# Attention's matmuls between those of the first product, and D^T G one step later

## The chip, the cores and the metric

The kernel runs on one core of one Trainium2 chip. The metric is the device time of one execution in microseconds (us). The kernel before takes 780.31 us in the median of 3 runs (776.99 to 781.22).

## The reference

```
attention, per batch and head, in chunks of 64 positions:
    scores = q_c @ k_c.T / sqrt(D);  scores -= max(scores, -1)
    attn = exp(scores) / (sum + 1e-9);  out = attn @ v_c
x = out as (4608, 512)
first layer:   h = max(x @ w_in, 0);  x = (h * h) @ w_out       (512 -> 2048 -> 512)
soft mixture:  logits = x @ phi                                 (32 slots, 8 experts)
    d = softmax over tokens;  slot_input = d.T @ x
    slot_out = max(slot_input @ w1[e], 0) @ w2[e]
    c = softmax over slots;   result = c @ slot_out
```

There are 8 batches, 8 heads, 576 positions and a head size of 64.

## The kernel before

The 4608 tokens are 36 tiles of 128 tokens (two chunks of 64). The tiles form blocks: one of 1, one of 2, then eleven of 3. A block goes through 16 steps, one for each strip of 128 columns of the first layer.

A step of block b and strip f does this: the first product, 12 matmuls of 384 columns in fp16 parts (`moe_h`, tile hps), relu and square on ACT, and, two steps later, three transpositions of the squares (`moe_turn`, gT), their copy out of PSUM into a tile G (`moe_keep`), and after every fourth strip the logits (`moe_logits`, L). The second layer is never formed by itself: w_out is folded into phi beforehand, and d.T @ x is got as D^T G, where G are the transposed squares. `soft(b)` is a generator that runs one stretch per step after a block's last logits: scaled logits (Ls), their sum (the product at L864, called l4), softmax over tokens (dts), softmax over slots, then the transposition of dts (L917) and dd (L919), and in the next step D^T G (L926, 24 rows of the trace), which is added to acc (L937).

The attention of tile i is a table of operations (`attention(i)`), each with an engine, the operations that it needs and a stage. In the order of time, with the names used below: loads of q, k, v (SyncE); `am`, the largest magnitudes (DVE L182); the reduction over partitions (PE L205, L206, called r1 below); scales (DVE L215, L218, L398); `hi` (ACT L405) and `lo` (DVE L410), the fp16 parts of q and k; T, a DMA transpose into qkT (L431); `vh` and `vl`, the parts of v (GpSimd L420, DVE L425); `qbd`, two copies of qkT (DVE L435); scores `qk`, 24 matmuls of 64 columns (L446 to L448); `mx` (DVE L452), `less` (DVE L455), exp (ACT L461), `su` (DVE L466), `rs` (DVE L468); normalisation (GpSimd L471); the parts of the probabilities (ACT L481, GpSimd L484); PT, a DMA transpose into pT (L487); the values product `pv`, 24 matmuls of 64 columns (L498 to L500); `xh` (ACT L504) and `xl` (DVE L510), the parts of the result in xb, the operand of the first product. Buffers come in pairs by the tile's parity, so the loads of tile i+2 wait until tile i is done with its own: v's until the second `vl`, q's until `hi` and `lo`.

Up to some 175 us a list scheduler in the kernel sets the order of all engines. Then the steady part begins. A tile's table is handed out by tokens: at step st + k its operations of stage k are written down, ahead of that step's first product. `st` is the tile's block's first step less 16, and 5 less for each tile that follows in the block. On TensorE the written order is the program's order:

```
        put_until(t + 1)
        ...
            moe_h(b, f)
            moe_relu(b, f)
            moe_square(b, f)
        ...
        for fn in slots.pop(t, []):
            fn()
```

On the other engines a scheduler at build time orders the instructions, and each engine works through its queue in that order. Of the eight banks of PSUM two are for hps, one for gT, two for logits (one of them later for gT as well), and three, called misc, are shared in turn by the attention and `soft`.

Of the kernel before, what the change touches and what calls it, by code (L numbers as in the profile page):

```python
# [37 lines left out]
N32 = 9  # L38


class Op:
# [9 lines left out]
        self.share = 0.0  # L51

    def __call__(self):
        self.fn(self.eng) if self.choose else self.fn()


def cost_of(kind, n):
# [17 lines left out]
def kernel(  # L75
# [25 lines left out]
    dve, act, pool, pe, sp = nc.vector, nc.scalar, nc.gpsimd, nc.tensor, nc.sync  # L101

    blocks = []
# [62 lines left out]
    ps_t = ps1.enter_context(tc.tile_pool(name="ps_t", bufs=1, space=PSUM))  # L166
    ps_h = ps1.enter_context(tc.tile_pool(name="ps_h", bufs=2, space=PSUM))
    ps_m = ps1.enter_context(tc.tile_pool(name="ps_m", bufs=1, space=PSUM))
    bank_of, n_misc, turn, held_banks = {}, [0], [None], {}

    def misc():
        x = bank_of.get(turn[0])
        if x is None:
            while n_misc[0] % 3 in held_banks:
                n_misc[0] += 1
            x = n_misc[0] % 3
            n_misc[0] += 1
        return ps_m.tile([P, 512], F32, tag=f"misc{x}", name="misc")

    def largest_of(src, am):  # L180
# [189 lines left out]
    def attention(i):  # L370
        b, j = tile_block[i]
# [6 lines left out]
        v, ops = {}, {}  # L378

        def old(*names):  # L380
            return [(("t", i - 2), n) for n in names]

        older = old
# [56 lines left out]
        def scores():  # L440
            qkT, qbd = qkT_b[par], qbd_b[par]
            kh = qkT[:, 8:12].rearrange("p a (h2 t) -> p (a h2) t", h2=2)
            kl = qkT[:, 12:16].rearrange("p a (h2 t) -> p (a h2) t", h2=2)
            v["sc"] = sc = misc().rearrange("p (h t) -> p h t", h=8)
            for h in range(8):
                pe.matmul(sc[:, h], qbd[:, 0, h], kh[:, h], start=True, stop=False)  # L446
                pe.matmul(sc[:, h], qbd[:, 0, h], kl[:, h], start=False, stop=False)
                pe.matmul(sc[:, h], qbd[:, 1, h], kh[:, h], start=False, stop=True)  # L448

        def largest():  # L450
            v["mx"] = sm.tile([P, 8], F32, tag="mx", name="mx", bufs=2)
            dve.tensor_reduce(out=v["mx"], in_=v["sc"], axis=AX.X, op=ALU.max)  # L452
# [36 lines left out]
        def pv():  # L489
            vbd, pT = vbd_b[par], pT_b[par]  # L490
            v["xq"] = misc()
            v["xp"] = xp = v["xq"].rearrange("p (a t) -> p a t", a=4)
            for y in range(8):
                c, hp = divmod(y, 4)
                o = xp[:, hp, 64 * c : 64 * c + 64]
                ph = pT[:, y // 2, 64 * (y % 2) : 64 * (y % 2) + 64]
                pl = pT[:, 4 + y // 2, 64 * (y % 2) : 64 * (y % 2) + 64]
                pe.matmul(o, vbd[:, 0, y], ph, start=True, stop=False)  # L498
                pe.matmul(o, vbd[:, 0, y], pl, start=False, stop=False)
                pe.matmul(o, vbd[:, 1, y], ph, start=False, stop=True)  # L500


        def xh():
# [43 lines left out]
        for c in range(2):  # L547
            ops[f"qd{c}"] = Op("dve", 0.44, ["T", *old("qk")], 6, lambda c=c: qdiag(c))
        ops["qk"] = Op("pe", 0.75, ["qd0", "qd1"], 8, scores)
        ops["max"] = Op("dve", 0.6, ["qk"], 8, largest)  # L550
        ops["less"] = Op(
            "dve", 0.6, ["max", *(old("phi", "plo") if i - 2 >= N32 else older("Tp"))], 8, less
        )
        ops["exp"] = Op("act", 0.72, ["less"], 9, exp)
        ops["sums"] = Op("dve", 1.03, ["exp"], 9, sums)
        ops["normal"] = Op({"pool": 1.2, "dve": 0.61}, None, ["sums"], 9, normal)
        ops["phi"] = Op({"act": 0.63, "pool": 0.8}, None, ["normal", *old("PT")], 10, phi_)
        ops["plo"] = Op("pool", 1.25, ["phi"], 10, plo)
        ops["PT"] = Op("dma", 0.9, ["plo", *old("pv")], 10, ptrans)
        ops["pv"] = Op("pe", 0.75, ["PT", "vl0", "vl1"], 14, pv)  # L560
        ops["xh"] = Op("act", 0.6, ["pv"], 14, xh)
        ops["xl"] = Op("dve", 0.6, ["xh"], 14, xl)
        for n in ("lo0", "lo1", "vl0", "vl1", "qd0", "qd1", "normal"):
            ops[n].share = 0.4
        return ops
# [150 lines left out]
    def cols(b):  # L716
        o0 = bank0.get(b, 0)
        return slice(o0 * P, (o0 + blocks[b][1]) * P)

    def moe_h(b, f):  # L720
        n = blocks[b][1] * P
        xb = xb_b[max(group[b], 1) % 2][:, :, :, cols(b)]
        hp = ps_h.tile([P, 512], F32, tag="h", name="hps")[:, :n]
        nm = 0
        for kt in range(KT):
            for wl, xl in ((0, 0), (0, 1), (1, 0)):
                pe.matmul(  # L727
                    hp, wi[f][:, wl, kt], xb[:, xl, kt], start=(nm == 0), stop=(nm == 3 * KT - 1)
                )
                nm += 1  # L730
        gt_ps[b, f] = hp

    def g_of(b, f):
        k = max(group[b], 1), f // QF
        if k not in g_q:
            g_q[k] = big.tile([P, QF, 3 * P], F32, tag=f"g{len(g_q) % 2}", name="g")
        return g_q[k][:, f % QF, cols(b)]

    def moe_relu(b, f, eng="act"):
        g, hp, sc = g_of(b, f), gt_ps.pop((b, f)), inv_w[:, f : f + 1]  # L740
        if eng == "act":
            act.activation(out=g, in_=hp, func=ACTF.Relu, scale=sc)  # L742
        else:
            dve.tensor_scalar(g, hp, sc, 0.0, ALU.mult, ALU.max)

    def moe_square(b, f, eng="act"):
        g = g_of(b, f)
        if eng == "act":
            act.activation(out=g, in_=g, func=ACTF.Square)  # L749
        else:  # L750
            (dve if eng == "dve" else pool).tensor_tensor(out=g, in0=g, in1=g, op=ALU.mult)
# [97 lines left out]
    def soft(b):  # L849
        s0, n = blocks[NB if b == 1 else b]  # L850
        last = s0 + n == NT
# [68 lines left out]
            out=dd, in0=tp, in1=iv.unsqueeze(2).to_broadcast([P, n, NS]), op=ALU.mult  # L920
        )
        yield
        y = misc()
        for j in range(n):
            for g in range(NQ):
# [176 lines left out]

    def emit(task, name, op):
        emitted.add((task, name))
        turn[0] = (task, name)
        op()
        turn[0] = None
        if (task, name) in bank_of:
            held_banks[bank_of[task, name]] = [(task, n) for n in gives[name]]
        for x, users in list(held_banks.items()):  # L1110
            if all(u in emitted for u in users):
                del held_banks[x]
# [8 lines left out]
    gives = {  # L1121
        "reduce": ("finish",), "wT": ("wTc",), "wp": ("wpc",), "T0": ("qd0", "qd1"), "T1": ("kc",), "qk": ("less",), "Tp": ("pc",), "pv": ("xl",)
    }
# [196 lines left out]
    def put_rest(t, turned=None):  # L1320
        n = sum(x[0] <= t_list + 2.0 + SLOT * t for x in rest)
        if turned:
            n = max([n] + [x + 1 for x, o in enumerate(rest) if o[2] in turned and o[3] in ("T", "lg")])
        for _, _, task, name, op in rest[:n]:
            if (task, name) not in emitted:
                emit(task, name, op)
        del rest[:n]
# [4 lines left out]
    first_use = {b: (b - 3) * NF + NF - fb for b in range(3, NB)}  # L1332
    tokens = []
    for i in range(9, NT):
        b, j = tile_block[i]
        st = first_use[b] - 16 - 5 * (blocks[b][1] - 1 - j)
        tokens.append((st - 5, len(tokens), i, -1))
        tokens += [(st + k, len(tokens) + k, i, k) for k in range(15)]
    tokens.sort()

    def put(i, stage):
# [10 lines left out]
    def put_until(t):  # L1352
        late = []
        while tokens and tokens[0][0] < t:
            x = tokens.pop(0)
            if not put(*x[2:]):
                late.append((t, *x[1:]))
        tokens.extend(late)
        tokens.sort()
# [34 lines left out]
    while t < end or any(x >= t for x in slots):  # L1394
        put_rest(t)
        put_until(t + 1)
        b, f = steps[t] if 0 <= t < len(steps) else (None, None)
        if b == 2 and f % QF == 0:
            put_rest(t, [("s", NB, x) for x in range(f, f + QF)])
        if b is not None:  # L1400
            moe_h(b, f)
            moe_relu(b, f)
            moe_square(b, f)
            if (b, f) == (NB - 1, NF - 1):
                give((big, f"xb{b % 2}", 1536))
        for fn in slots.pop(t, []):
            fn()
        if b == NB - 1 and f % 2:
            give((big, f"wi{f // 2}", 1024))
        if 0 <= t - LAG < len(steps):  # L1410
            b, f = steps[t - LAG]
            moe_turn(b, f)
            moe_keep(b, f)
            if f % QF == QF - 1:
                moe_logits(b, f // QF)
            if f == NF - 1:
                if b == NB - 1:
                    give((big, "g0", 1536))
                gen = soft(b)
                run_gen(t + 1 if b < NB - 1 else t, gen)  # L1420
                if b == NB - 1:
                    slots[t].pop()()
        t += 1
# [220 lines left out]
```

## Time and profile before

| | us |
|---|---|
| median of 3 runs | 780.31 (776.99 to 781.22) |
| profiled execution | 778.18 |
| its span | 776.4 |
| TensorE busy | 707.2 (91%) |
| DVE busy | 431.7 (56%) |
| ACT busy | 457.1 (59%) |
| GpSimd busy | 167.4 (22%) |

In the trace an engine's row gives the start in us from the span's beginning, the duration, the engine, the line, the operation and its tiles. A matmul's duration is longer than the distance to the next one, since they overlap; distances between starts tell what TensorE spends. In brackets stands how long the engine was idle before, and what ended it.

### The profile page before, as it was taken

The page shows a single profiled execution, that of the slowest core. Times are in us where ns is not written, and L with a number is a line of the kernel's source. Part 1 is how long each engine was busy: PE and PEld are TensorE (multiplying, and loading weights), DVE is VectorE, ACT ScalarE, POOL GpSimd, SP SyncE. Part 2 cuts the span into 40 slices and gives each one's busy share as a digit, 9 for nine tenths or more (in the row PEclk, how much of TensorE's full clock was granted, in tenths as well). Part 3 has the DMA queues.
Part 4 walks back from the last instruction along what each step waited for, and adds up shares of the span by engine and source line. Part 5 has one row for each costly group of instructions (what it writes and reads, how often), then busy time and mean ns, then how long its engine had stood idle before and what let it go on. Part 6 is the DMA issues. An engine that isn't in the chain of part 4 may idle for free.

```text
span 776.4 us, 16693 instructions
## 1 busy us (share of the span) xinstructions
PE 707.2 (91%) x6612; PEld 456.1 (59%) x6612; DVE 431.7 (56%) x908; ACT 457.1 (59%) x951; POOL 167.4 (22%) x209
## 2 busy tenths in 40 slices
PE   5788999889999999998999989999999999969790
PEld 4677776665566565665666656656566565524350
DVE  4799996367666565656566566656565301022160
ACT  3688887554666565656676556656566655531150
POOL 3332211131223222223122222322232200030000
PEclk9899999999999999999999999999999999999995
DMA  7896934234364544543544737444567423669998
GB/s 155 215 279 161 217 120 139 66 66 87 81 137 92 98 83 83 123 96 69 109 96 89 100 62 142 86 96 83 82 90 184 150 83 117 227 214 356 349 353 255
DMA packets 242589, 110.47 MB, mean 142 GB/s; under 512 B 201808, under 2 KB 235600, under 8 KB 242512
## 3 DMA queue, kind: packets, MB, share of 16 engines
q1 hardware_dynamic: 242512, 109.41, 58.0%
q8 instruction: 52, 0.85, 0.5%
q14 instruction: 25, 0.20, 0.1%
HBM read 78.71 MB, written 9.44 MB: 114 GB/s over the span
## 4 chain that ended last, share of the span: by engine, by line
PE 65%; DMA 14%; DVE 12%; ACT 3%; issue 2%; SPq 1%; POOL 1%; DVEq 0%; POOLq 0%; ACTq 0%
PE hps L727 38%; PE gT L761 7%; PE L L778 4%; PE misc L926 4%; DMA unit<-in_moe_w_dram 3%; DMA qkT<-qk 3%; DMA qkv<-in_v_dram 2%; PE ehps L1466 2%; DVE qk L276 2%; DMA qkv<-in_q_dram 2%; DMA qkv<-in_k_dram 2%; DMA pT<-p 1%; DVE am L182 1%; DVE vbd L425 1%; DVE stage L281 1%
## 5 line engine op out<-in xcount | busy, mean ns | idle before, releaser
L727 PE MATMUL hps<-xb,wi 128*128 128x384 f16 (+2 forms) x2400 | 407.8, 320 | 0.5 <-ACT g L742 0.2
L727 PEld LDWEIGHTS <-wi 128*128 128x128 f16 x2400 | 224.9, 98 | 138.8 <-issue 17.6
L742 ACT ACTIVATE g<-hps,inv_w 128x384 f32<-128x384 f32 (+1 forms) x200 | 112.7, 563 | 98.4 <-PE hps L727 96.6
L188 ACT ACTIVATE G<-gT 128x384 f32<-128x384 f32 (+1 forms) x200 | 94.2, 471 | 33.8 <-PE gT L761 30.6
L182 DVE TENSOR_REDUCE am<-qkv 128x1 bf16<-128x512 f32 x90 | 61.9, 687 | 83.6 <-DMA qkv<-in_v_dram 31.9
L761 PE MATMUL gT<-ident,g 128*128 128x128 f32 x576 | 98.1, 277 | 4.0 <-ACT G L188 3.1
L749 ACT ACTIVATE g<-g 128x384 f32<-128x384 f32 (+2 forms) x188 | 96.8, 515 | 1.5
L761 PEld LDWEIGHTS gT<-ident,g 128*128 128x128 f32 x576 | 73.0, 144 | 28.8 <-issue 10.4
L420 POOL TENSOR_SCALAR vbd<-qkv,as 64x512 f16<-64x512 f32 x54 | 41.7, 772 | 97.2 <-PE misc L500 81.5
L471 POOL TENSOR_TENSOR ex<-ex,rs 128x512 f32<-128x512 f32 x27 | 29.3, 1085 | 103.4 <-DVE rs L468 93.0
L410 DVE SCALAR_TENSOR_TENSOR qk<-qkv,as,qk 128x512 f16<-128x512 f32 x54 | 39.4, 756 | 20.8 <-ACT qk L405 20.3
L425 DVE SCALAR_TENSOR_TENSOR vbd<-qkv,as,vbd 64x512 f16<-64x512 f32 x54 | 47.3, 876 | 1.0
L405 ACT ACTIVATE qk<-qkv,as 128x512 f16<-128x512 f32 x54 | 36.8, 716 | 10.7 <-DVE as L215 10.7
L778 PE MATMUL L<-g,wp 128*32 128x384 f32 x384 | 41.7, 498 | 0.0
L926 PE MATMUL misc<-G,dd 128*32 128x512 f32 x288 | 33.4, 596 | 7.2 <-DVE dd L919 6.6
L484 POOL TENSOR_TENSOR p<-ex,p 128x512 f16<-128x512 f32 x27 | 34.9, 1292 | 21.7 <-ACT p L481 21.7
L481 ACT ACTIVATE p<-ex 128x512 f16<-128x512 f32 x27 | 17.0, 630 | 35.5 <-POOL ex L471 35.5
L223 POOL TENSOR_SCALAR iv_all<-ai 128x1 f32<-128x1 f32 x27 | 7.5, 276 | 118.5 <-DVE ai L218 117.6
L435 DVE COPY qbd<-qkT 64x1024 f16<-64x1024 f16 x54 | 22.7, 420 | 17.3 <-DMA qkT<-qk 16.5
L510 DVE SCALAR_TENSOR_TENSOR xb<-misc,xb 128x512 f16<-128x512 f32 x27 | 18.1, 671 | 25.1 <-ACT xb L504 24.8
L461 ACT ACTIVATE ex<-ex,es 128x512 f32<-128x512 f32 x27 | 19.4, 718 | 19.4 <-DVE ex L455 19.4
L854 DVE TENSOR_TENSOR Ls<-L,iv_all 128x384 f32<-128x384 f32 x12 | 6.6, 553 | 41.0 <-PE L L778 40.8
(156 smaller groups left out, 1018.7 us busy)
## 6 DMA issues: line engine op xcount, KB each, us to landing
unit<-in_moe_w_dram SPq DMA_DIRECT2D x34, 512.0 KB, 4.5
unit<-in_moe_w_dram SPq DMA_DIRECT2D x60, 256.0 KB, 6.0
qkv<-in_q_dram SPq DMA_DIRECT2D x72, 128.0 KB, 3.4
qkv<-in_k_dram SPq DMA_DIRECT2D x72, 128.0 KB, 3.3
qkv<-in_v_dram SPq DMA_DIRECT2D x72, 128.0 KB, 3.4
stage<-in_moe_w_in_dram SPq DMA_DIRECT2D x16, 512.0 KB, 5.1
stage<-in_moe_w_out_dram SPq DMA_DIRECT2D x16, 512.0 KB, 5.8
out_dram<-o SPq DMA_DIRECT2D x14, 512.0 KB, 6.3
```

Source lines behind the costliest of these rows:

```text
L182: dve.tensor_reduce(out=am, in_=src, axis=AX.X, op=ALU.max, apply_absolute_value=True)
L188: act.activation(out=out, in_=in_, func=ACTF.Copy)
L405: act.activation(out=qk16[:, 2 * a], in_=flat[:, a], func=ACTF.Copy, scale=v["s"][:, a : a + 1])
L410: dve.scalar_tensor_tensor(out=qk16[:, 2 * a + 1], in0=flat[:, a], scalar=v["s"][:, a : a + 1], in1=qk16[:, 2 * a], op0=ALU.mult, op1=ALU. ...
L420: pool.tensor_scalar(out=dst[0], in0=vin, scalar1=v["s"][pr, 2:3], scalar2=1.0, op0=ALU.mult, op1=ALU.mult,)
L425: dve.scalar_tensor_tensor(out=dst[1], in0=vin, scalar=v["s"][pr, 2:3], in1=dst[0], op0=ALU.mult, op1=ALU.subtract,)
L727: pe.matmul(hp, wi[f][:, wl, kt], xb[:, xl, kt], start=(nm == 0), stop=(nm == 3 * KT - 1))
L742: act.activation(out=g, in_=hp, func=ACTF.Relu, scale=sc)
L749: act.activation(out=g, in_=g, func=ACTF.Square)
L761: pe.transpose(gt_ps[b, f][:, j], g[:, j * P : (j + 1) * P], ident)
L778: pe.matmul(L_ps[g0][NS * x : NS * x + NS, :n], wp[:, QF * q + x], g[:, x, :n], start=(q == 0), stop=(q == NQ - 1), tile_position=(0, NS * x),
L926: pe.matmul(y[NS * g : NS * g + NS], dd[:, j], G_q[b, g][:, j], start=(j == 0), stop=(j == n - 1), tile_position=(0, NS * g), skip_group_c ...
```

## The change

`scores` and `pv` of the fp16 tiles become generators: `yield` stands after the second and, in odd heads, after the third matmul of a head. `emit` starts such a generator and keeps it in `lazy`; `moe_h` lets each one go on after every matmul of the first product. An operation that needs one which is still going on drains it first, and after the first product what is left is drained. The stages of `mx`, `less`, the normalisation, `xh` and `xl` go up by one, tiles start one step earlier (17 and 16 stages instead of 16 and 15), `soft` yields once more ahead of D^T G, and `misc` passes over a bank that a tile's operation still holds.

```
-        self.fn(self.eng) if self.choose else self.fn()
+        return self.fn(self.eng) if self.choose else self.fn()
...
-        if x is None:
+        if x is None or x in held_banks:
+            assert len(held_banks) < 3
...
                 pe.matmul(sc[:, h], qbd[:, 0, h], kl[:, h], start=False, stop=False)
+                yield
                 pe.matmul(sc[:, h], qbd[:, 1, h], kh[:, h], start=False, stop=True)
+                if h % 2:
+                    yield
...
-        ops["max"] = Op("dve", 0.6, ["qk"], 8, largest)
+        ops["max"] = Op("dve", 0.6, ["qk"], 9, largest)
...
-        ops["xh"] = Op("act", 0.6, ["pv"], 14, xh)
+        ops["xh"] = Op("act", 0.6, ["pv"], 15, xh)
...
                 nm += 1
+                for me, gen in list(lazy.items()):
+                    if next(gen, lazy) is lazy:
+                        del lazy[me]
...
+        if not last and b > 1:
+            yield
         y = misc()
...
-        op()
+        made = op()
+        if made is not None:
+            lazy[task, name] = made
+            next(made)
...
-        st = first_use[b] - 16 - 5 * (blocks[b][1] - 1 - j)
+        st = first_use[b] - 17 - 5 * (blocks[b][1] - 1 - j)
         tokens.append((st - 5, len(tokens), i, -1))
-        tokens += [(st + k, len(tokens) + k, i, k) for k in range(15)]
+        tokens += [(st + k, len(tokens) + k, i, k) for k in range(16)]
...
             moe_h(b, f)
+            for me in list(lazy):
+                list(lazy.pop(me))
```

What moves on TensorE, first at a D^T G in the steady part (a block's third tile). Before, D^T G stands behind the first product that follows the transposition of dts, and the scores of a tile come behind it in one piece:

```order
L727 MATMUL hps<-xb_86,wi_1140 128x384
L926 MATMUL misc<-G,dd 32x512 x12
L761 MATMUL gT<-ident,g 128x128 x3
L446 LDWEIGHTS qbd
L446 MATMUL misc<-qkT,qbd 128x64
L447 LDWEIGHTS qbd
L447 MATMUL misc<-qkT,qbd 128x64
L448 LDWEIGHTS qbd
L448 MATMUL misc<-qkT,qbd 128x64
```

In the changed kernel the scores are spread over that first product (wi_1140), and the values product of another tile over the next one (wi_1310), behind which D^T G now stands:

```order
L451 LDWEIGHTS qbd
L451 MATMUL misc<-qkT,qbd 128x64
L737 LDWEIGHTS wi_1140
L737 MATMUL hps<-xb_86,wi_1140 128x384
L774 MATMUL gT<-ident,g 128x128 x3
L503 LDWEIGHTS vbd
L503 MATMUL misc<-pT,vbd 128x64
L504 LDWEIGHTS vbd
L504 MATMUL misc<-pT,vbd 128x64
L737 LDWEIGHTS wi_1310
L737 MATMUL hps<-xb_86,wi_1310 128x384
```

So one, two or three short matmuls stand between two of the first product, and D^T G is one step further from dd.

On DVE, at the first tile of a block (tile 18; qk_81 and qkv_79 belong to the odd tiles, 19 and 21, and ex_82 to tile 18), the rows before are these: `lo` of 19, `xl` of 17, `mx` of 18, `vl`, `am` of 21's q, `vl`, `less` of 18.

```order
L410 SCALAR_TENSOR_TENSOR qk_81<-qkv_79,as,qk_81 128x512 x2
L510 SCALAR_TENSOR_TENSOR xb_86<-misc,xb_86 128x4x128
L452 TENSOR_REDUCE mx<-misc 128x8
L425 SCALAR_TENSOR_TENSOR vbd<-qkv_79,as,vbd 64x8x64
L182 TENSOR_REDUCE am<-qkv_79 128x1
L425 SCALAR_TENSOR_TENSOR vbd<-qkv_79,as,vbd 64x8x64
L455 TENSOR_TENSOR ex_82<-misc,mx 128x512
L435 COPY qbd<-qkT 64x16x64 x2
```

And in the changed kernel:

```order
L412 SCALAR_TENSOR_TENSOR qk_81<-qkv_79,as,qk_81 128x512 x2
L184 TENSOR_REDUCE am<-qkv_79 128x1
L457 TENSOR_REDUCE mx<-misc 128x8
L427 SCALAR_TENSOR_TENSOR vbd<-qkv_79,as,vbd 64x8x64
L518 SCALAR_TENSOR_TENSOR xb_86<-misc,xb_86 128x4x128
L460 TENSOR_TENSOR ex_82<-misc,mx 128x512
L427 SCALAR_TENSOR_TENSOR vbd<-qkv_79,as,vbd 64x8x64
L437 COPY qbd<-qkT 64x16x64 x2
```

`am` of the new q moved ahead of `mx`, `xl` behind the first `vl`, and the second `vl` behind `less`.

On DVE, at the second tile of the same block (tile 19; qk_80 and qkv_78 belong to the even tiles, ex_83 to 19), before:

```order
L410 SCALAR_TENSOR_TENSOR qk_80<-qkv_78,as,qk_80 128x512 x2
L452 TENSOR_REDUCE mx<-misc 128x8
L455 TENSOR_TENSOR ex_83<-misc,mx 128x512
L182 TENSOR_REDUCE am<-qkv_78 128x1
L466 TENSOR_REDUCE su<-ex_83 128x8
L874 TENSOR_REDUCE rm<-misc 128x1
L467 TENSOR_SCALAR su<-su 128x8
L435 COPY qbd<-qkT 64x16x64
```

And in the changed kernel:

```order
L412 SCALAR_TENSOR_TENSOR qk_80<-qkv_78,as,qk_80 128x512 x2
L867 TENSOR_TENSOR Ls<-L,iv_all 128x384
L457 TENSOR_REDUCE mx<-misc 128x8
L437 COPY qbd<-qkT 64x16x64 x2
L460 TENSOR_TENSOR ex_83<-misc,mx 128x512
L184 TENSOR_REDUCE am<-qkv_78 128x1
L427 SCALAR_TENSOR_TENSOR vbd<-qkv_78,as,vbd 64x8x64
L518 SCALAR_TENSOR_TENSOR xb_87<-misc,xb_87 128x4x128
L427 SCALAR_TENSOR_TENSOR vbd<-qkv_78,as,vbd 64x8x64
L471 TENSOR_REDUCE su<-ex_83 128x8
```

The copies `qbd` of tile 20 moved ahead of `less` of tile 19, and `xl` and both `vl` ahead of its `su`.

## Rows read from the trace of the kernel before

**Rows 1.** The page: busy us, share of the span, instructions.
```profile
PE 707.2 (91%) x6612; PEld 456.1 (59%) x6612; DVE 431.7 (56%) x908; ACT 457.1 (59%) x951; POOL 167.4 (22%) x209
```

**Rows 2.** Windows, 190 to 676: length, busy (count) of PE, PEld, DVE, ACT, POOL, clock, DMA.
```profile
190.00:676.00 486.00, 477.41 (x4335) 300.33 (x4334) 267.34 (x587) 301.98 (x641) 110.75 (x130) 1.00 0.51 105
```

**Rows 3.** Waits of TensorE, 190 to 676: us in total, times, longest us.
```profile
PE misc L926 <- DVE dd L919: 6.6, 4, 2.0
PE misc L498 <- DMA pT<-p: 1.3, 3, 0.6
```

**Rows 4.** Timeline of TensorE, tile 18: start, us, engine, line, operation.
```profile
321.92 0.17 PE L205 MATMUL misc<-am,ones 128*128 128x3 bf16 x1
...
325.84 0.19 PE L446 MATMUL misc<-qkT,qbd 128*128 128x64 f16 x1
...
326.54 2.12 PE L727 MATMUL hps<-xb,wi 128*128 128x384 f16 x12
328.49 0.49 PE L761 MATMUL gT<-ident,g 128*128 128x128 f32 x3
...
341.52 0.81 PE L864 MATMUL misc<-Ls,sel 128*128 128x384 f32 x2
342.16 0.49 PE L761 MATMUL gT<-ident,g 128*128 128x128 f32 x3
342.60 0.19 PE L498 MATMUL misc<-pT,vbd 128*128 128x64 f16 x1
```

**Rows 5.** Groups by line, weight loads: busy us, mean ns, idle before.
```profile
L446 PEld LDWEIGHTS <-qbd 128*128 128x128 f16 x216 | 19.4, 98 | 0.1
```

**Rows 6.** Timeline of DVE, first tile of the block (18).
```profile
326.67 0.69 DVE L510 SCALAR_TENSOR_TENSOR xb<-misc,xb 128x512 f16<-128x512 f32 x1 [1.40 <-ACT xb L504]
327.28 0.68 DVE L452 TENSOR_REDUCE mx<-misc 128x8 f32<-128x512 f32 x1
327.88 0.73 DVE L425 SCALAR_TENSOR_TENSOR vbd<-qkv,as,vbd 64x512 f16<-64x512 f32 x1
328.54 0.67 DVE L182 TENSOR_REDUCE am<-qkv 128x1 bf16<-128x512 f32 x1
329.25 0.75 DVE L425 SCALAR_TENSOR_TENSOR vbd<-qkv,as,vbd 64x512 f16<-64x512 f32 x1
330.03 0.69 DVE L455 TENSOR_TENSOR ex<-misc,mx 128x512 f32<-128x512 f32 x1
...
335.23 0.69 DVE L182 TENSOR_REDUCE am<-qkv 128x1 bf16<-128x512 f32 x1 [0.33 <-DMA qkv<-in_v_dram]
...
336.03 0.20 DVE L468 RECIPROCAL rs<-su 128x8 f32<-128x8 f32 x1
```

**Rows 7.** Timeline of DVE, second tile of the block (19).
```profile
340.02 1.41 DVE L410 SCALAR_TENSOR_TENSOR qk<-qkv,as,qk 128x512 f16<-128x512 f32 x2 [2.47 <-ACT qk L405]
...
342.07 0.69 DVE L455 TENSOR_TENSOR ex<-misc,mx 128x512 f32<-128x512 f32 x1
344.83 0.69 DVE L182 TENSOR_REDUCE am<-qkv 128x1 bf16<-128x512 f32 x1 [2.07 <-DMA qkv<-in_q_dram]
345.43 0.68 DVE L466 TENSOR_REDUCE su<-ex 128x8 f32<-128x512 f32 x1
...
348.25 0.42 DVE L435 COPY qbd<-qkT 64x1024 f16<-64x1024 f16 x1 [1.60 <-DMA qkT<-qk]
```

**Rows 8.** DMA transposes by line: T (L431), from issue to landing.
```profile
DMA to landing us min/median/max: 4.3/4.7/6.4
```

**Rows 9.** DMA transposes by line: PT (L487), from issue to landing.
```profile
DMA to landing us min/median/max: 3.1/3.3/5.0
```

**Rows 10.** Timeline of SyncE's queue: issue of PT for tile 19.
```profile
352.64 1.25 SPq L487 DMA_TRANSPOSE pT<-p  x1
```

**Rows 11.** Timeline of TensorE, D^T G and `pv` of tile 19.
```profile
356.79 2.78 PE L926 MATMUL misc<-G,dd 128*32 128x512 f32 x24 [2.05 <-DVE dd L919]
359.51 0.55 PE L761 MATMUL gT<-ident,g 128*128 128x128 f32 x3
...
362.92 0.19 PE L498 MATMUL misc<-pT,vbd 128*128 128x64 f16 x1
```

More of the change, by code (lines that the diff above doesn't have):

```diff
@@ L168 @@
     ps_m = ps1.enter_context(tc.tile_pool(name="ps_m", bufs=1, space=PSUM))
-    bank_of, n_misc, turn, held_banks = {}, [0], [None], {}
+    bank_of, n_misc, turn, held_banks, last_bank = {}, [0], [None], {}, [0]
     def misc():
         x = bank_of.get(turn[0])
-        if x is None:
+        if x is None or x in held_banks:
+            assert len(held_banks) < 3
             while n_misc[0] % 3 in held_banks:
@@ L177, in misc @@
             n_misc[0] += 1
+        last_bank[0] = x
         return ps_m.tile([P, 512], F32, tag=f"misc{x}", name="misc")
@@ L499, in pv @@
                 pe.matmul(o, vbd[:, 0, y], pl, start=False, stop=False)
+                yield
                 pe.matmul(o, vbd[:, 1, y], ph, start=False, stop=True)
+                if y % 2:
+                    yield
         def xh():
@@ L549, in attention @@
         ops["qk"] = Op("pe", 0.75, ["qd0", "qd1"], 8, scores)
-        ops["max"] = Op("dve", 0.6, ["qk"], 8, largest)
+        ops["max"] = Op("dve", 0.6, ["qk"], 9, largest)
         ops["less"] = Op(
-            "dve", 0.6, ["max", *(old("phi", "plo") if i - 2 >= N32 else older("Tp"))], 8, less
+            "dve", 0.6, ["max", *(old("phi", "plo") if i - 2 >= N32 else older("Tp"))], 9, less
         )
@@ L555, in attention @@
         ops["sums"] = Op("dve", 1.03, ["exp"], 9, sums)
-        ops["normal"] = Op({"pool": 1.2, "dve": 0.61}, None, ["sums"], 9, normal)
+        ops["normal"] = Op({"pool": 1.2, "dve": 0.61}, None, ["sums"], 10, normal)
         ops["phi"] = Op({"act": 0.63, "pool": 0.8}, None, ["normal", *old("PT")], 10, phi_)
@@ L560, in attention @@
         ops["pv"] = Op("pe", 0.75, ["PT", "vl0", "vl1"], 14, pv)
-        ops["xh"] = Op("act", 0.6, ["pv"], 14, xh)
-        ops["xl"] = Op("dve", 0.6, ["xh"], 14, xl)
+        ops["xh"] = Op("act", 0.6, ["pv"], 15, xh)
+        ops["xl"] = Op("dve", 0.6, ["xh"], 15, xl)
         for n in ("lo0", "lo1", "vl0", "vl1", "qd0", "qd1", "normal"):
@@ L718, in cols @@
         return slice(o0 * P, (o0 + blocks[b][1]) * P)
+    lazy = {}
     def moe_h(b, f):
@@ L922, in soft @@
         yield
+        if not last and b > 1:
+            yield
         y = misc()
@@ L1104, in emit @@
         emitted.add((task, name))
+        for d in op.deps:
+            d = d if isinstance(d, tuple) else (task, d)
+            if d in lazy:
+                list(lazy.pop(d))
         turn[0] = (task, name)
-        op()
+        made = op()
+        if made is not None:
+            lazy[task, name] = made
+            next(made)
         turn[0] = None
-        if (task, name) in bank_of:
-            held_banks[bank_of[task, name]] = [(task, n) for n in gives[name]]
+        if name in gives:
+            held_banks[last_bank[0]] = [(task, n) for n in gives[name]]
         for x, users in list(held_banks.items()):
```

## The prediction

> **What bounds the kernel now.** I read the page first, then the busy time of the steady stretch, then who TensorE waited for there, and last the order of time of one period of a block, engine by engine. The page shows TensorE busy for 91% of the span [rows 1]. In the steady stretch, from 190 to 676 us, it is busy for 477.41 of 486.00 us at the full granted clock, 2.4 GHz [rows 2]: only 8.6 us can be had there. The list of waits names most of it: D^T G waits 6.6 us for dd in four places, and the values product (`pv`) waits 1.3 us for the transposed probabilities in three [rows 3]. So a change of the order can win about 8 us in this stretch, while it can lose as much as it makes TensorE wait.
>
> **The change part by part.**
>
> *Spreading the bursts.* 27 tiles have two bursts of 24 matmuls of 64 columns. In block 18 to 20 (tiles 18, 19, 20) the burst of scores starts at 325.84 and the first product's own first matmul follows at 326.54: 0.70 us for 24, 29 ns each [rows 4]. That last step is a change from a short matmul to a long one with new weights, and it costs nothing above 29 ns. The change makes 12 such passages per burst instead of one, 648 in 54 bursts, and the same number the other way. The loads of these weights last 98 ns by their own record [rows 5], yet matmuls start 29 ns apart, so the loads run ahead. Bounds: if each of the 648 passages laid bare what a load has beyond 29 ns, 69 ns, that were 45 us lost; if a spread matmul cost nothing at all, 38 us (54 x 0.70) won. I take 0, because the one row of such a passage shows no price.
>
> The Trainium skill ("TensorE: Matmul & The Clock Gate", LDWEIGHTS) prices a weight load by its columns over 1.2 GHz, 107 ns for 128 columns. As an estimate by that page a burst would be bound by its loads at 24 x 107 ns = 2.6 us and spreading would save some 1.9 us each time, about 100 us in all; the burst of 0.70 us contradicts this as a spacing, so the sum goes without it.
>
> *D^T G one step later.* It moves behind the next step's first product (1.95 us), a transposition and a burst, some 3 us. The longest wait for dd in the list is 2.0 us [rows 3], so I count all 6.6 us as won. The ring of G has seven buffers and a block uses four; the fifth to seventh are filled by the next block's first twelve steps, so the later reading holds nobody up.
>
> *The tiles' new stages.* A tile begins one step earlier; scores, and all before them, come one step earlier, but end only with the product that they are spread over. The softmax keeps its step. The values product comes one step earlier. So what stands between scores and values product shrinks by a step on TensorE, less what the earlier scores give. What decides is DVE, whose queue goes in order, and there the change puts other instructions first (the order rows in the section on the change). The Trainium skill ("PSUM — Partial Sum Buffer", Engine vs sequencer instructions) calls the queues of ScalarE, VectorE and GpSimd strictly first in, first out. The trace agrees: an `am` waits 2.07 us for its load, and `su`, whose tile had been through `less` at 342.76, comes at 345.43 right behind it [rows 7]. If DVE could pass a waiting instruction, the result would be that of the first rival below.
>
> *First tile of a block* (18, with r1 at 321.92 as zero; r1 is the PE reduction for tile 19). Before, DVE did `mx` at +5.4, and the load-dependent `am` at +6.6 without a wait; the second `vl`, which frees the buffer for tile 21's v, ended at +8.1; `am` of that v load came at +13.3 after a short wait, `rs` ended at +14.3, and `pv` started at +20.7 with no wait worth listing [rows 6, 4]. In the change `am` for the new q stands ahead of `mx`. q is asked for when `lo` of tile 19 is done, a fixed time after r1, so `am` can again start only near +6.6. Behind it come `mx`, `vl`, `xl`, `less`, `vl`. By the spacing of the same rows these and `am` take 0.71 + 0.60 + 0.66 + 0.61 + 0.70 + 0.78 = 4.1 us, so the second `vl` ends at +10.7 instead of +8.1. The v load is then issued and lands about 4 us later (before, 330.00 to 335.23 was 5.2 us, of which a part was SyncE's own queue). `am` for v still stands ahead of `rs`: `rs` ends near +15.5, 1.2 us later than before. From the end of `rs` to `pv` it was 342.60 - 336.23 = 6.4 us without slack, so `pv` can start at +21.9. TensorE gets there earlier than before by the l4 product (342.16 - 341.52 = 0.64 us), which now stands behind it: at +20.0. New wait: about 1.8 us, in every block.
>
> *Second tile* (19). Before, `less` came right behind `mx` and ended 6.5 us after the first tile's `rs` (342.76 - 336.23). In the change the two `qbd` copies of the third tile stand between them, and these wait for that tile's transpose: `lo` for it ended 5.2 us after `rs` (341.43) [rows 7], the transpose lands 4.7 us after its issue in the median [rows 8] and is issued some 0.4 us after `lo`, then `qbd` 0.85 and `less` 0.7: 11.8 us after `rs`, or +27.3. From the end of `less` to the issue of the probabilities' transpose it was 352.64 - 342.76 = 9.9 us, 8.3 without the 1.60 us for which `qbd` stood there, and 3.3 more to landing [rows 7, 9, 10]: +38.9. TensorE: `pv` to `pv` was 362.92 - 342.60 = 20.3 us [rows 4, 11]; without D^T G (359.51 - 356.79 = 2.7) and its wait of 2.05, and with l4's 0.64, it is 16.2, in blocks without small waits nearer 15.4. From +21.9 that is +37.3 to +38.1. New wait: 0.8 to 1.6, I take 1.4 because most blocks have no such small waits.
>
> *The third tile* gains: its scores no longer stand behind D^T G, and I count 0. GpSimd and SyncE keep their orders, but for a third of the tiles the q load's second half stands behind a transpose, inside the times above.
>
> *Sum.* Seven full blocks (tiles 12 to 32): 7 x (1.8 + 1.4) = 22.4 us of new waits. Won: 6.6 for dd and 1.3 of `pv` waits that the new ones contain, 7.9. Net +14.5 us on the profiled execution's own 778.18, so 792.7. The median of the runs shown, 780.31, is 2.1 above that execution; on it the sum is 794.8. Forecast: 795.
>
> **The rivals.**
>
> *The waits go and none comes* (faster). For it: the whole pipeline starts a step earlier, and the second tile's `pv` had its transpose some 7 us ahead (352.64 + 3.3 against 362.92). Against it: the first tile had no slack. It gives 780.3 - 7.9 = 772.
>
> *Only the first tile's wait comes* (the second tile's lead is enough): 7 x 1.8 - 7.9 = +4.7, 785. It decides on whether the third tile's transpose lands before `mx` of the second ends.
>
> *The passages between short and long matmuls cost something* (slower): at 69 ns each 825, at a third of it 795 without any new wait. Against it stands the row at 326.54.
>
> *A late load drags further* (slower): where `less` is late, exp, which stands in ACT's queue ahead of the relu of a step, holds that relu and with it the PSUM buffer of the first product. It decides as soon as `less` of the second tile ends more than two steps (4.6 us) behind its scores, at some 2 us per block: 7 x 2 = 14 more, 809.
>
> *The change leaves the time as it was*: the new waits are half of mine (11) and take back the 7.9: 783.
>
> *The load-bound burst of the page named above* would give some 680; the burst of 0.70 us leaves it a chance that rounds to 0.
>
> **How the numbers follow.** This kernel can tell about 0.5%, 3.9 us, from no change. Chances: forecast 0.45 (slower); late load 0.10 (slower); costly passages 0.05 (slower); first tile only 0.12, at the bound, a third of it counted slower and the rest the same; unchanged 0.06; waits gone 0.22 (faster). That is 0.64 slower, 0.14 the same, 0.22 faster. The likeliest case alone spans 786 (A wait of 1 us each, half of the second) to 806 (loads late by the 1 to 2 us that the transposes' 4.3 to 6.4 us show). The range reaches down to 772, the rival with no wait, and up to 811, the late load.
>
> **What would show it.** If I am right, the list of waits after has no dd row, and `pv` waits for pT some 20 us in about 14 places, 1 to 2 us each; the first product's matmuls still follow each other at 0.16 us and the short ones add 0.03 us each; `am` waits for q ahead of `mx`, and `qbd` for qkT ahead of `less`. I am wrong about spreading if the 12 matmuls with 24 between take other than 2.65 us. I am wrong about the lead if the waits for pT stay under 5 us.

## The result and the profile after

The changed kernel is slower: 787.84 us in the median (785.64 to 792.75) against 780.2 (776.65 to 782.94), ratio 1.0104 (95% interval 1.0071 to 1.0138). A second measurement beside other runs gave 1.0081 (1.0055 to 1.0108). The forecast was 795. So the direction holds, and the loss that was forecast, 15 us, is nearly twice the measured one: +8 us by the ratio, 785.2 - 776.4 = +8.8 us by the two profiled spans.

The page of the changed kernel, busy us of each engine, answers to [rows 1]: TensorE does the same 6612 matmuls in the same busy time, in a longer span.

```profile
PE 707.8 (90%) x6612; PEld 454.2 (58%) x6612; DVE 423.5 (54%) x908; ACT 455.4 (58%) x951; POOL 156.8 (20%) x209
```

The steady stretch, same columns as [rows 2]. TensorE is 473.68 us busy instead of 477.41 at the same clock: 3.7 us more idle.

```profile
190.00:676.00 486.00, 473.68 (x4299) 296.88 (x4298) 257.65 (x588) 296.13 (x632) 100.82 (x129) 1.00 0.49 102
```

What TensorE waited for there, as in [rows 3]: the row for dd is gone. Waits of the first product for relu have come, which I had only as a rival, and those for pT have grown from 1.3 to 4.3 us, not to 20. I had set waits under 5 us as the sign that I am wrong about the lead of `pv`, and so I was.

```profile
PE hps L737 <- ACT g L755: 6.9, 8, 1.9
PE misc L503 <- DMA pT<-p: 4.3, 5, 1.5
```

To divide the loss I took the distances between the starts of TensorE's matmuls, with the first product as a ruler (12 matmuls a step, so step n begins with its matmul 12n). They also hold the short waits that the list leaves out. Up to step 32 (some 140 us) the kernels differ by 0.3 us and from step 196 to the end by 0.03 (109.38 and 109.41). Between them:

| stretch | before | after | difference |
|---|---|---|---|
| steps 32 to 52 (start of the steady part) | 80.83 | 83.67 | +2.84 |
| steps 52 to 196: after matmuls of the first product (waits of D^T G for dd) | 289.85 | 283.00 | -6.84 |
| steps 52 to 196: after transpositions (waits for relu's bank or pT) | 54.05 | 67.07 | +13.02 |
| steps 52 to 196 in all | 446.16 | 451.83 | +5.67 |

A second pair of traces of the same two kernels (runs 11 and 5 below) divides alike, with other sizes: +4.4, -9.0, +11.8 and +2.6.

**What a spread step costs.** The timeline of TensorE where the first product carries two bursts (`pv` of 17 and scores of 18), its start and its end:

```profile
328.42 0.19 PE L503 MATMUL misc<-pT,vbd 128*128 128x64 f16 x1
...
328.51 0.19 PE L449 MATMUL misc<-qkT,qbd 128*128 128x64 f16 x1
328.54 0.33 PE L737 MATMUL hps<-xb,wi 128*128 128x384 f16 x1
328.70 0.19 PE L506 MATMUL misc<-pT,vbd 128*128 128x64 f16 x1
...
331.58 0.19 PE L451 MATMUL misc<-qkT,qbd 128*128 128x64 f16 x1
331.61 0.33 PE L737 MATMUL hps<-xb,wi 128*128 128x384 f16 x1
331.77 0.49 PE L774 MATMUL gT<-ident,g 128*128 128x128 f32 x3
```

From a long matmul to the next start it is 0.16 us, from a short one 0.03, and the whole is 331.77 - 328.42 = 3.35 us: 1.95 + 2 x 0.70, what the pieces take one after the other. It also shows the other side: the scores of 18 are complete at 331.6, where with both bursts ahead of the product they would be at 328.42 + 1.40 = 329.8.

**The second tile.** The clearest block is that of tiles 24 to 26. DVE, with the scores of the second tile (25) just done:

```profile
446.38 0.69 DVE L457 TENSOR_REDUCE mx<-misc 128x8 f32<-128x512 f32 x1 [0.63 <-PE misc L451]
451.86 0.86 DVE L437 COPY qbd<-qkT 64x1024 f16<-64x1024 f16 x2 [4.79 <-DMA qkT<-qk]
452.75 0.69 DVE L460 TENSOR_TENSOR ex<-misc,mx 128x512 f32<-128x512 f32 x1
```

ACT in the same time:

```profile
447.80 0.60 ACT L512 ACTIVATE xb<-misc 128x512 f16<-128x512 f32 x1
453.47 0.72 ACT L466 ACTIVATE ex<-ex,es 128x512 f32<-128x512 f32 x1 [5.07 <-DVE ex L460]
454.10 0.56 ACT L755 ACTIVATE g<-hps,inv_w 128x384 f32<-128x384 f32 x1
```

And TensorE:

```profile
450.39 2.11 PE L737 MATMUL hps<-xb,wi 128*128 128x384 f16 x12
452.34 0.49 PE L774 MATMUL gT<-ident,g 128*128 128x128 f32 x3
454.71 2.11 PE L737 MATMUL hps<-xb,wi 128*128 128x384 f16 x12 [1.88 <-ACT g L755]
```

Read from the top: `qbd` of the third tile waits 4.79 us for its transpose; `less` of the second stands behind it; exp waits 5.07 us for `less`; relu stands behind exp in ACT's queue; and the second product after the one that relu reads needs its bank, and waits 1.88 us. The Trainium skill ("PSUM — Partial Sum Buffer", Engine vs sequencer instructions) calls these queues strictly first in, first out; this trace agrees twice, at 452.75 and at 454.10.

**The first tile** (18, r1 at 326.09). DVE, answering to [rows 6]:

```profile
332.30 0.69 DVE L184 TENSOR_REDUCE am<-qkv 128x1 bf16<-128x512 f32 x1 [2.95 <-DMA qkv<-in_q_dram]
332.90 0.68 DVE L457 TENSOR_REDUCE mx<-misc 128x8 f32<-128x512 f32 x1
...
334.76 0.67 DVE L460 TENSOR_TENSOR ex<-misc,mx 128x512 f32<-128x512 f32 x1
335.46 0.75 DVE L427 SCALAR_TENSOR_TENSOR vbd<-qkv,as,vbd 64x512 f16<-64x512 f32 x1
...
339.20 0.69 DVE L184 TENSOR_REDUCE am<-qkv 128x1 bf16<-128x512 f32 x1 [0.58 <-DMA qkv<-in_v_dram]
339.80 0.19 DVE L473 RECIPROCAL rs<-su 128x8 f32<-128x8 f32 x1
```

TensorE at its values product, answering to the end of [rows 4]:

```profile
345.52 0.33 PE L737 MATMUL hps<-xb,wi 128*128 128x384 f16 x1
345.69 0.49 PE L774 MATMUL gT<-ident,g 128*128 128x128 f32 x3
346.27 0.19 PE L503 MATMUL misc<-pT,vbd 128*128 128x64 f16 x1
```

The queue is as forecast: `am` for q ahead of `mx`, the second `vl` ends at +10.1. But `am` for the v load came at +13.1, where it was +13.3 before, `rs` ended at +13.9 instead of the +15.5 that I reckoned, and pT landed at +20.14. Three transpositions take 0.33 us where nothing is awaited (0.11 each by the starts), so TensorE could have begun `pv` at 346.02, +19.9; it began at +20.2, right behind the landing.

### The profile page after: what moved, and what is told of

Same layout as the page of the kernel before. It is cut to its first block, busy times and chain, and to the rows that moved or that the text cites. A ratio compares the mean times of both kernels' runs of the same rounds, so it can differ in the third digit from the quotient of the medians.

```text
span 785.2 us, 16693 instructions
## 1 busy us (share of the span) xinstructions
PE 707.8 (90%) x6612; PEld 454.2 (58%) x6612; DVE 423.5 (54%) x908; ACT 455.4 (58%) x951; POOL 156.8 (20%) x209
## 3 DMA queue, kind: packets, MB, share of 16 engines
q1 hardware_dynamic: 242512, 109.41, 57.3%
## 4 chain that ended last, share of the span: by engine, by line
PE 56%; DMA 18%; DVE 13%; ACT 5%; POOL 2%; issue 2%; SPq 1%; DVEq 0%; POOLq 0%; ACTq 0%
PE hps L737 32%; PE gT L774 6%; DMA qkT<-qk 5%; PE misc L941 4%; PE L L791 3%; DMA qkv<-in_q_dram 3%; DMA unit<-in_moe_w_dram 3%; DMA qkv<-in_v_dram 3%; DMA pT<-p 2%; PE ehps L1490 2%; DVE qk L278 2%; DVE am L184 1%; DVE ex L460 1%; DVE qk L277 1%; POOL p L489 1%
## 5 line engine op out<-in xcount | busy, mean ns | idle before, releaser
L737 PE MATMUL hps<-xb,wi 128*128 128x384 f16 (+2 forms) x2400 | 435.4, 320 | 6.9 <-ACT g L755 6.9
L422 POOL TENSOR_SCALAR vbd<-qkv,as 64x512 f16<-64x512 f32 x54 | 37.6, 697 | 127.7 <-PE misc L504 70.1
L448 PE MATMUL misc<-qkT,qbd 128*128 128x64 f16 x216 | 41.5, 195 | 0.0
L437 DVE COPY qbd<-qkT 64x1024 f16<-64x1024 f16 x54 | 24.3, 450 | 31.9 <-DMA qkT<-qk 31.1
L449 PE MATMUL misc<-qkT,qbd 128*128 128x64 f16 x216 | 41.5, 195 | 0.0
L451 PE MATMUL misc<-qkT,qbd 128*128 128x64 f16 x216 | 41.4, 194 | 0.0
L427 DVE SCALAR_TENSOR_TENSOR vbd<-qkv,as,vbd 64x512 f16<-64x512 f32 x54 | 40.5, 751 | 0.9
L503 PE MATMUL misc<-pT,vbd 128*128 128x64 f16 x216 | 35.0, 193 | 4.8 <-DMA pT<-p 4.3
L489 POOL TENSOR_TENSOR p<-ex,p 128x512 f16<-128x512 f32 x27 | 31.3, 1161 | 20.5 <-ACT p L486 20.5
```

What stands on the lines that cost most here:

```text
L427: dve.scalar_tensor_tensor(out=dst[1], in0=vin, scalar=v["s"][pr, 2:3], in1=dst[0], op0=ALU.mult, op1=ALU.subtract,)
L737: pe.matmul(hp, wi[f][:, wl, kt], xb[:, xl, kt], start=(nm == 0), stop=(nm == 3 * KT - 1))
```

## The experiments

All ratios are to the kernel before, run beside them; intervals are 95%.

**1. D^T G one step later alone** (the kernel before with one more `yield`).

```
         yield
+        if not last and b > 1:
+            yield
         y = misc()
```

> The kernel before with D^T G one step later and nothing else. Theory (the later D^T G wins all its waits and costs nothing): TensorE no longer waits for dd, 6.8 us less by the distances between starts from step 52 to step 196; about 773.4 against 780.2, ratio 0.991; the waits of pv for pT stay at 1 to 2 us. Rival (another chain of the same block is as late as dd and takes the wait over): 778 to 780, and a new row of waits of 4 us or more stands in the place of dd.

Measured 773.74 us, ratio 0.9856 (0.9819 to 0.9893). What TensorE waited for from 190 to 676 us (its longest row):

```profile
PE misc L498 <- DMA pT<-p: 1.4, 2, 0.8
```

Nothing took the place of dd. From step 52 to 196 it takes 440.41 us, 5.75 less than the first trace of before; the measured time fell by 11 us, more than expected, which run 11 takes up. It is the fastest kernel of the study, and beats both the kernel before and the changed one.

**2. The spreading without the later D^T G.**

```
-        if not last and b > 1:
-            yield
         y = misc()
```

> The changed kernel with D^T G back at its old step. Theory (two separate effects: 6.8 us won by D^T G, 13 us of new waits for relu and pT in the steady part and 3 us at its start lost by the rest): the waits for dd come back on top of the others, 787.8 + 6.8 = 794.6, by their overlap with the new waits 791 to 797. Rival (the waits for relu already hide what dd needs, so D^T G decides nothing here): 787 to 789.

801.64 us, 1.0211 (1.017 to 1.0251). By the ratio (1.0211 x 780.2 = 796.7) the size was inside what I expected, the way was not: no wait for dd came back, and the two other waits doubled. From 250 us on dd is ready at most 2.6 us after the transposition of dts begins, where it took up to 5.0 in the first trace of before; and D^T G comes later, mostly 3.3 us after that transposition, since the spread scores of the third tile stand ahead of it. Why the other waits doubled is not shown.

```profile
PE hps L737 <- ACT g L755: 12.9, 13, 2.5
PE misc L503 <- DMA pT<-p: 8.9, 13, 1.1
```

**3. Both bursts whole, at the new stages.**

```
-            lazy[task, name] = made
-            next(made)
+            list(made)
```

> The changed kernel with each burst whole again, ahead of the step's first product, at the new stages. In it DVE has less of a block's second tile ahead of the copies qbd of the third. Theory (less behind qbd is what holds exp, relu and the bank of hps): the 13 us of new waits fall to 5 or less, the 6.8 of dd stay won, the 3 us at the start of the steady part stay: 776 to 782. Rival 1 (the values product a step earlier has too short a lead, whatever the order on DVE): the wait goes to pT, 787 to 790. Rival 2 (nothing of the loss hangs on the spreading): the same rows as after, 787.8.

782.44 us, 0.9968 (0.9944 to 0.9993). The waits for pT are gone; of the 11.2 us of waits for relu and pT in the list of the changed kernel 6.0 stay, all for relu:

```profile
PE hps L737 <- ACT g L755: 6.0, 10, 1.1
```

So the step earlier of `pv` is not too short a lead, and about 1% hangs on the spreading. Which of its two effects, the order on DVE or the later end of the scores, this run does not tell.

**4. The third tile of each block at its old step.**

```
-        st = first_use[b] - 17 - 5 * (blocks[b][1] - 1 - j)
+        st = first_use[b] - 17 - 5 * (blocks[b][1] - 1 - j) + (j == 2)
```

> The changed kernel, spread as it is, with the third tile of each block starting one step later (its old place). In it DVE has less of the second tile ahead of qbd of the third. Theory (the order on DVE, not the spreading): the waits of hps for relu fall from 7 to 8 us to under 2, those for pT stay under 5; 776 to 782. Rival 1 (spreading by itself holds the scores back and with them exp and relu): the waits for relu stay, 786 to 789. Rival 2 (the third tile now becomes late for its own values product): waits for pT of 1 to 2 us in each of eight blocks, 786 to 794.

799.29 us, 1.017 (1.0128 to 1.0212). My theory missed: with `less` ahead of `qbd` again it is slower than the changed kernel. It moves too much at once: the third tile loses a step, and steps 32 to 52 alone took 90.85 us (83.67 in the changed kernel). By size (1.017 x 780.2 = 793.5) and by the waits for pT it looks like the second rival, but these waits stand at the first and second tiles of the blocks; the third tile, which that rival made late, has its pT 2.31 us ahead in the median. So what lost the time here stays open.

```profile
PE misc L503 <- DMA pT<-p: 8.5, 12, 2.7
PE gT L774 <- ACT G L190: 3.9, 1, 3.9
PE hps L737 <- ACT g L755: 3.9, 6, 1.3
```

**5. The changed kernel again**, beside runs 6 to 8.

> The changed kernel once more, as the yardstick for the runs beside it. Expected by its first measurement: ratio 1.0104 to before (1.007 to 1.014).

790.53 us, 1.0081 (1.0055 to 1.0108).

**6. `qbd` held behind `less`.**

```
+            if tile_block[i][1] == 1 and i > 12:
+                for c in range(2):
+                    pr = slice(64 * c, 64 * c + 64)
+                    dve.tensor_copy(qbd_b[1 - par][pr, 0, 0, 64 * c : 64 * c + 1], ex[pr, 0:1])
```

> The changed kernel, in which less of a block's second tile is followed on DVE by two copies of one column of its result into qbd of the third tile; the copies qbd overwrite these, so they can only come behind less. The order on TensorE and all else on DVE stay. Theory (qbd waiting for the transpose ahead of less holds exp, exp holds relu in ACT's queue, and relu holds the bank of hps): the waits of hps for relu fall from 8.2 us to 2 or less, those for pT stay at 4 to 7, so 4 to 8 us are won: ratio to before 1.000 to 1.006. Rival (the scores come 2 us later through the spreading, and exp is late by itself, whatever the order): waits for relu stay over 5 us, 1.008 to 1.013.

794.96 us, 1.0144 (1.0118 to 1.017). Half of the theory holds: no wait of TensorE for relu is left in the list. But the time went up.

```profile
PE misc L507 <- DMA pT<-p: 9.2, 13, 1.2
PE misc L207 <- DVE cmat L917: 5.0, 7, 1.9
```

DVE in the same block as above:

```profile
451.67 0.69 DVE L457 TENSOR_REDUCE mx<-misc 128x8 f32<-128x512 f32 x1 [0.24 <-PE misc L451]
452.39 0.69 DVE L460 TENSOR_TENSOR ex<-misc,mx 128x512 f32<-128x512 f32 x1
453.12 0.33 DVE L467 CAST qbd<-ex 64x1 f16<-64x1 f32 x2
458.68 0.69 DVE L184 TENSOR_REDUCE am<-qkv 128x1 bf16<-128x512 f32 x1 [5.23 <-DMA qkv<-in_q_dram]
459.28 0.86 DVE L437 COPY qbd<-qkT 64x1024 f16<-64x1024 f16 x2
...
462.33 0.69 DVE L475 TENSOR_REDUCE su<-ex 128x8 f32<-128x512 f32 x1
```

`less` now comes at once, and DVE stands 5.23 us one place further, at `am`, ahead of the same `su`: from `mx` to `su` it is 10.7 us here and 9.7 in the changed kernel, so `rs` is no earlier, and pT isn't either. The edit moved more than I had said: the scheduler also put this `am` ahead of `qbd`. So here `less` ahead of `qbd` changed who waits and won nothing; what it would do with `am` left behind `qbd`, this run does not tell.

**7. Only the values product spread.**

```
-            lazy[task, name] = made
-            next(made)
+            if name == "qk":
+                list(made)
+            else:
+                lazy[task, name] = made
+                next(made)
```

> The changed kernel with the values product spread and the scores as a whole burst ahead of the first product, at the new stages. DVE has less of the second tile ahead of qbd of the third, and less of the first ahead of both vl. Theory (what costs is that spread scores end 2 us later; a spread values product costs nothing, since xb is not needed before the next block): as with both in bursts, 0.993 to 1.000. Rival (spreading of either kind costs): 1.002 to 1.008.

777.33 us, 0.9919 (0.9895 to 0.9943), against 1.0081 with the scores spread too: 1.6% hang on the spread scores, more than the whole loss of the change. With both bursts whole it was 0.9968 (run 3), so the spread values product by itself costs nothing and may win some 0.5%; the list has 2.2 us of waits for relu here and 6.0 there. DVE's order differs between the two, and why it wins is not shown. The largest row of waits left:

```profile
PE hps L737 <- ACT g L755: 2.2, 4, 1.0
```

**8. The first block of the steady part (tiles 9 to 11) at its old step.**

```
-        st = first_use[b] - 17 - 5 * (blocks[b][1] - 1 - j)
+        st = first_use[b] - 17 - 5 * (blocks[b][1] - 1 - j) + (i < 12)
```

> The changed kernel with tiles 9 to 11, the first block of the steady part, starting at their old step. Theory (at the start of the steady part loads, am and qbd of the tiles a step earlier stand on DVE ahead of cm and cmat of the first soft, which frees a bank for the last fp32 values product): the wait of 4.4 us there falls to about 1.5 and the drop of the clock at 175 to 180 us goes; 3 us less than the changed kernel, 1.0065. Rival (the time is given back in the first block, whose own loads then come later): 1.009 to 1.012.

790.66 us, 1.008 (1.0054 to 1.0106): the same as run 5. What it was to remove did go. TensorE at the last fp32 values product, in the kernel before:

```profile
174.21 1.15 PE L661 MATMUL misc<-pT,vbd 128*64 128x64 f32 x32 [1.35 <-DVE cmat L900]
```

in the changed kernel:

```profile
176.71 1.65 PE L669 MATMUL misc<-pT,vbd 128*64 128x64 f32 x32 [4.23 <-DVE cmat L913]
```

and here:

```profile
175.07 1.15 PE L669 MATMUL misc<-pT,vbd 128*64 128x64 f32 x32 [0.92 <-DVE cmat L913]
```

Yet steps 32 to 52 take 83.67 us in both. Against the changed kernel steps 36 to 40 take 5.8 us less (this wait, and a mean granted clock of 1.00 in place of 0.71 from 175 to 180 us), steps 40 to 44 1.5 more, and steps 46 to 50 2.6 more; so far the rival holds, the time is given back in the first block. The last 1.6 us, more in steps 32 to 36, go with the clock at another place, where executions differ: from 150 to 160 us its mean was 0.83 here and 1.00 in the changed kernel, but 0.67 in run 5 of the same kernel. The 2.6 us are in the main another wait: the transposition behind D^T G, at the same time in both kernels, waits for the copy of G 0.56 us in the changed kernel and 3.15 here.

```profile
215.81 0.55 PE L774 MATMUL gT<-ident,g 128*128 128x128 f32 x3 [0.56 <-ACT G L190]
```

```profile
216.06 0.55 PE L774 MATMUL gT<-ident,g 128*128 128x128 f32 x3 [3.15 <-ACT G L190]
```

**9. The scores as a whole burst behind the first product** (the values product still spread).

```
-                    if next(gen, lazy) is lazy:
+                    if me[1] == "pv" and next(gen, lazy) is lazy:
...
             lazy[task, name] = made
-            next(made)
+            if name == "pv":
+                next(made)
```

> The changed kernel with the scores as one whole burst right behind the step's first product, so that they end when the spread ones end; the values product stays spread. Theory (what costs is only that the scores end some 2 us later than ahead of the product, which eats the 2.3 us that pv has in hand): no slack between the landing of pT and pv in first tiles, as in the changed kernel, and a ratio of 1.003 to 1.012. Rival (the interleaving itself costs, by short matmuls among long ones or by the scheduler's order on DVE for it): the slack of 2 us and 0.992, as with the scores ahead.

796.91 us, 1.016 (1.0126 to 1.0195), though DVE has `less` of the second tile ahead of `qbd` here. The scores are not interleaved at all and end late, and the loss is there, larger than I expected. So interleaving is not what costs, and neither is `qbd` ahead of `less`. What the run does not hold still is the rest of DVE's order: `am` for the next q comes ahead of the first tile's `mx`, as in the changed kernel.

```profile
PE misc L503 <- DMA pT<-p: 10.0, 11, 2.1
PE hps L737 <- ACT g L755: 4.2, 8, 0.9
```

The time that `pv` has in hand, from the landing of pT to the start of `pv` (medians in us of seven tiles each, 12 to 32, from the traces). At 0.04 to 0.14 nothing is in hand: `pv` starts as soon as pT has landed.

| kernel | first tile | second | third |
|---|---|---|---|
| before | 0.37 | 6.89 | 2.60 |
| D^T G later alone (1) | 0.54 | 5.72 | 5.61 |
| both whole, new stages (3) | 2.32 | 4.29 | 4.86 |
| only `pv` spread (7) | 2.34 | 4.30 | 5.05 |
| changed | 0.04 | 0.14 | 1.20 |
| scores behind the product (9) | 0.14 | 0.14 | 0.80 |

A step of the first product is 1.95 us, and ending the scores behind it takes that from every tile. The first tile loses 2.65 in the changed kernel, since the spread values product of the tile before shares its product (3.35 against 0.70); from its last scores to the landing of pT it is 14.7 us there and in run 7 alike. In the second tile this way is 17.6 us against 13.6 in run 7: 4.0 us more, gone in the queues on the way, on top of the 1.95, and 4.3 were in hand.

**10. Only `pv` spread, and tiles 9 to 11 at their old step** (the edits of 7 and 8).

> The kernel with the values product spread, scores whole and ahead, D^T G a step later, and tiles 9 to 11 at their old step. Theory (the 3 us at the start of the steady part are a separate loss that comes back here, where later tiles have slack): 0.992 less 0.004, 0.986 to 0.990. Rival (given back in the first block, as it was without this slack): 0.991 to 0.994.

777.87 us, 0.9924 (0.9897 to 0.995): as 7, so the rival again.

**11. The kernel before, for its trace.**

> The kernel before, for its trace beside those of the other runs. The later D^T G alone gave 1.4% against 6.8 us (0.9%) by the first trace of before. If that trace was a mild one, the waits for dd here are 9 us or more; if they are 6 to 7 again, the rest is not in the steady part.

783.96 us. The waits for dd are a third more than in [rows 3], in seven places instead of four:

```profile
PE misc L926 <- DVE dd L919: 8.9, 7, 2.1
PE misc L498 <- DMA pT<-p: 2.1, 3, 0.8
```

From step 52 to 196 it takes 450.12 us, so run 1 is 9.7 us faster there: that is most of its 11 us (784.97 to 773.74).

## Why the prediction was right in direction, and half wrong in size

*What bounds the kernel*: right. The win is a few us, the loss what TensorE is made to wait.

*Spreading costs nothing by itself*: right, to 0.01 us per step; only there are fewer passages from short to long than I counted, 434 instead of 648. In part this is because `vh` of the third tile needs `pv` of the first and drains it, and so the first tile's values product stays whole; in part because in eight steps two bursts share one product and its passages. The burst bound by its weight loads, which I had worked out from the Trainium skill ("TensorE: Matmul & The Clock Gate", LDWEIGHTS), has no part here: the 3.35 us above are the sum of the parts, and there was nothing for the spreading to hide.

*D^T G later wins its waits*: right, 6.84 us by the first pair of traces against 7.9 for dd and pT together, and 9.7 in run 1 against the trace of run 11. It is the only row of the table above that gains.

*First tile, 1.8 us per block*: this is the step that failed, by its size. I had the second `vl` at +10.7 (it was +10.1) and took the v load to land 4 us later; I priced its way from `vl` to landing by the 5.2 us of tile 18, a part of which I had myself put down to SyncE's queue. In the changed kernel `vl` ends at 336.21 and `am` of that load starts 3.0 us later. `rs` came at +13.9, and pT landed at +20.14, where I had +21.9; TensorE was there at +19.9, forecast +20.0. So the slack is used up in all seven blocks, as forecast, but the wait is 0.3 us in this block and 3.3 us in the seven by the starts, not 12.6.

*Second tile, 1.4 us per block*: `less` ended 11.45 us after the first tile's `rs` (tile 19: 351.45 against 340.00), forecast 11.8. But two thirds of the wait fell on relu's bank, ahead of `pv`: the mechanism of the rival "a late load drags further", in about one place a block, 8.3 us by the starts from step 52 to 196 against 1.0 before, where I gave it 14 on top of the rest. The rival's condition was met by my own figures, `less` at +27.3 and the scores done right ahead of the first tile's `pv` at +20.0, more than 4.6 us before; I gave it 0.10. I had treated the two as adding up. I read them as one lateness seen in two places, where what TensorE loses at relu it does not lose again at `pv`; run 6 fits that, where the waits for relu went and those for pT rose. At the seven second tiles' `pv` 3.7 us are lost, where 9.8 were forecast, and at all of `pv` 7.0 us against 1.3 before. The new waits are 7.3 + 5.7 = 13.0 us, where 22.4 were forecast.

*The start of the steady part*: not in the sum at all, and +2.84 us (+4.4 by the traces of 5 and 11). A tile that begins a step earlier puts its `am`, `qbd` and `vl` on DVE ahead of cm and cmat, which free the bank of the last fp32 values product (4.23 us in place of 1.35). In runs 8 and 10 this wait was taken away and the time stayed as it was, so its share is not settled.

*The sum*: -6.8 + 13.0 + 2.8 = +9.0; the other groups take 0.2 off and 8.8 are seen. Forecast: -7.9 + 22.4 = +14.5.

*The cause*: I put the loss down to DVE's order, the second tile's to `qbd` ahead of `less`. Runs 4, 6 and 9 have `less` first and are all slower than the changed kernel. Run 7 shows that the loss hangs on the spread scores, and run 9 that with late scores and no interleaving the loss is all there. What costs is that the scores are complete some 2 us later, in a chain that had 2.3 us in hand in the first tile, and that loses another 4.0 us in the queues in the second. No run has late scores with run 7's order on DVE, so how much of the second part is the lateness itself and how much the order that the scheduler makes of it stays open. So does why the scores behind the product cost more (1.016) than the spread ones (1.008) when both are complete only behind the product.

## What to carry to other kernels

Spreading a burst over a longer product took TensorE as long here as the two one after the other, and it delays the burst's last result by the length of the product; so do it only for products whose reader is not next in a chain (here the values product, not the scores). Of a change with several parts, run each alone: here one `yield` by itself (0.986) beat the whole change (1.010). And take one wait out of a full in-order queue only after looking at which instruction will stand there next.

## What was not expected of the hardware

After 4.23 us of idle time the granted clock was 0.71 in the mean of 175 to 180 us in the changed kernel; there matmuls of 64 columns followed each other at 0.053 us instead of 0.029, the lower level of 1.2 instead of 2.4 GHz:

```profile
175.00:180.00 5.00, 3.29 (x58) 3.01 (x59) 3.55 (x11) 1.96 (x4) 0.00 (x0) 0.71 0.23 52
```

Two executions of one kernel differ in where they wait: 6.6 us for dd in four places and 8.9 in seven. A gain that is read off one trace has that uncertainty.
